# Values' matmuls between the query groups, expert pieces loaded ahead of their casts, and small tiles turned in two PSUM banks, in a fused attention and mixture-of-experts kernel on one Trainium2 core

## The chip, the cores and the metric

The kernel runs on one core of a Trainium2 chip. The metric is the device time of one execution in microseconds, as the median of several runs. The engines are TensorE (PE, with its weight loads PEld), VectorE (DVE), ScalarE (ACT), GpSimd (POOL) and SyncE (SP); each works its own queue in order, and they signal each other.

## The reference

Three stages, each on the output of the one before: linear attention with an exponential feature map, a mixture of eight experts that sends each token to one expert, and a feed-forward with SiLU. All inputs are float32; 4 batches x 8 heads x 576 positions x 64 give 2304 tokens of 512.

```python
def phi(x):
    proj = np.einsum('bhsd,df->bhsf', x, w_phi)
    proj = proj - np.max(np.abs(proj), axis=-1, keepdims=True)
    return np.concatenate([np.exp(proj), np.exp(-proj)], axis=-1)
q_p, k_p = (phi(q), phi(k))
kv = np.einsum('bhsf,bhsd->bhfd', k_p, v)
z = np.sum(k_p, axis=2)
num = np.einsum('bhsf,bhfd->bhsd', q_p, kv)
den = np.einsum('bhsf,bhf->bhs', q_p, z)[..., None] + 1e-06
x = num / den
...
e_idx = np.argmax(x @ w_gate, axis=1)
...
for e in range(E):
    h = np.maximum(x[mask] @ w1[e], 0.0)
    out[mask] = gate_w[mask, None] * eom[mask, e, None] * (h @ w2[e])
...
h = x @ w_in
g = h * (1.0 / (1.0 + np.exp(-h)))
return (g @ w_out).astype(np.float32)
```

## The kernel before

**Attention** (`attention`, lines 75 to 357) walks eight units: two heads of two batches, nine tiles of 128 tokens. Per unit, `project` (114) multiplies three tiles at a time by `w_phi` into one of two alternating PSUM buffers (`pj`); VectorE takes the maximum out of it (L129) and subtracts (L130), which frees the buffer. There are three groups for the keys and three for the queries. `exp_k` (134) takes the keys' exponentials on ScalarE. `kv` (141) multiplies them by the values in steps of 20 and 16 TensorE instructions; the values' tile of a unit (`load_v`, 109) is one buffer. `turn_q` (157) transposes the queries on TensorE and takes their exponentials. `attend` (172) multiplies them by the values' sums and divides on VectorE (L191 to L193). Three PSUM banks (`pm`) go round among `turn_q`, `attend`, the gate's steps and the routing.

The loop at line 292 writes the order of TensorE, VectorE, ScalarE and GpSimd out by hand; only SyncE's queue is ordered by the scheduler. In a unit come query groups 0 and 1, the values' steps with pieces of other work between (`other`, 261), query group 2, the turns; then the next unit's keys between this unit's attend steps. From unit 4 on `other` carries the gate and the routing of the first half of the tokens: `decide`, `route.most` (426, which counts tokens per expert and picks the leading one), `route.ranks`, the early tokens' list, their rows, their transposes. `first_expert` (247) brings the leading expert's weights in 16 pieces: each call loads one piece (`wst`, four buffers), casts it on ScalarE (L258) and subtracts on GpSimd (L259).

**Experts** (`Moe`, 627 to 934). Weights and inputs are kept as a high and a low part, so each product is three matmuls. An early tile of 416 tokens comes first, then up to 16 tiles of 256 tokens; tiles 1 to 8 (`t < SURE`) always run, later ones under a condition. `one(t)` (891) has two conditional blocks, each with a preferred branch for full tiles (`first`, `second`) and another for tiles at most half full (`first_small`, `flip`, `second_small`). Between them and after them stand the transposes of the next tile's rows (`turn`), the casts of the next expert's weights (`new_first`, `new_second`), the refills of the weights' staging buffers by 2 MB transfers (`refill`) and, in tile 8, `route.compact_tokens`, which makes the list by which the last stage stores its rows. PSUM has four banks for hidden sums (`hidden`), two for second sums (`result`), two for transposes (`turned`). `second_small` (785) makes two halves of 256 columns, turns them into one `turned` bank and evicts each half as a high part on ScalarE (L840) and a low part on VectorE (L841). `banks` (759) says which banks the small tiles' first product and its turn use. Here tiles 2, 4, 8 and 11 take the small branch; tiles 9 and 10 are full; 12 and later are not used.

**Feed-forward** (`ffn`, from 1008): loads its rows by GpSimd (`Ready.load`, L1005) and runs two products per group of 384 tokens. The first such load is issued behind tile 8, ahead of the scaling of tile 10's rows (L722) in GpSimd's queue.

Of the kernel before, what the change touches and what calls it, by code (L numbers as in the profile page):

```python
# [7 lines left out]
F32 = mybir.dt.float32  # L8
# [11 lines left out]
B, H, S, D = 4, 8, 576, 64  # L20
# [11 lines left out]
SURE = 1 + -(-(NTOK - T0) // TW)  # L32
# [42 lines left out]
def attention(tc, c, k, qT, kT, v, w_phi, w_gate, w_ogate, w1, w2, w, xs, route, early_tile):  # L75
    nc = tc.nc
# [5 lines left out]
    sm = c.enter_context(tc.tile_pool(name="a_s", bufs=4))  # L82
# [16 lines left out]
    st = {}  # L99
# [134 lines left out]
    def gate(bp, n):  # L234

        for _ in range(n):
            f, i = GATE[st.get(("gate", bp), 0)]
            f(bp, i)
            st["gate", bp] = st.get(("gate", bp), 0) + 1
# [4 lines left out]
        V.memset(t[:, :, 1:], 0.0)  # L244
        store_x(bp, DM, t)

    def first_expert(n):

        i0 = st.get("piece", 0)
        st["piece"] = i0 + n  # L250
        if i0 == 0:
            st["e"] = nc.values_load(route.r["first"][0:1, 0:1], engines=[ENG.SP], min_val=0, max_val=NE - 1)
        for i in range(i0, min(i0 + n, 16)):
            name, src, f = ("w1", w1, i) if i < 8 else ("w2", w2, i - 8)
            t = sm.tile([128, 512], F32, name="wst", bufs=4)
            nc.sync.dma_start(out=t, in_=src[bass.ds(st["e"], 1), :, f * 512:(f + 1) * 512].rearrange("e p f -> (e p) f"))
            hi, lo = w[name + "h"][:, f * 512:(f + 1) * 512], w[name + "l"][:, f * 512:(f + 1) * 512]
            nc.scalar.copy(hi, t)  # L258
            nc.gpsimd.tensor_sub(lo, t, hi.bitcast(F32))  # L259

    def other(u, n):

        if u == H // 2:
            gate(0, (2, 2, 2, 2, 1, 1, 1)[n])
            if n == 6:
                decide(0)
        if u == H // 2 + 1:
            if n == 0:
                st["tile0"] = early_tile(pm)
                route.ranks(0, pm.tile([128, 512], F32, name="pm"), sm.tile([128, UT * NE], F32, name="rtmp", bufs=1))  # L270
            elif n == 3:
                st["tile0"].slots()
            elif n == 6:
                st["tile0"].tokens()
        if u > H // 2 and n in (1, 3, 5, 6):
            first_expert(1)
        if u == H // 2 + 2 and n == 1:
            st["tile0"].scale()
        if (u, n) in TURNS:
            st["tile0"].turn(TURNS.index((u, n)))  # L280
# [11 lines left out]
    for u in range(NU):  # L292
        bp, hp = divmod(u, H // 2)
        last = u == NU - 1
        if not last:
            load(u + 1, "k")
        project(u, "q", 0)
        project(u, "q", 1)
        kv(u, 0, 0, 0)
        other(u, 0)  # L300
        kv(u, 0, 0, 1)
        kv(u, 0, 1, 0)
        other(u, 1)
        kv(u, 0, 1, 1)
        project(u, "q", 2)
        other(u, 2)
        kv(u, 1, 0, 0)
        turn_q(u, 0)
        turn_q(u, 1)
        other(u, 3)  # L310
        kv(u, 1, 0, 1)
        other(u, 4)
        kv(u, 1, 1, 0)
        turn_q(u, 2)
        turn_q(u, 3)
        other(u, 5)
        kv(u, 1, 1, 1)
        turn_q(u, 4)
        other(u, 6)
        if last:  # L320
            first_expert(1)
            lc.close()
            kc.close()
            break
        load(u + 1, "q")
        load_v(u + 1)
        for g in range(NG):
            for p in ((0, 1), (), (2,))[g]:
                project(u + 1, "k", p)
            attend(u, g)  # L330
            exp_k(u + 1, 3 * g, 3 * g + 3)
            if u == H // 2 and g == 1:
                route.most(pm.tile([128, 512], F32, name="pm"))
            if u > H // 2 and g:
                first_expert(1)
            if u == H // 2 - 1 and g:
                gate(0, 2)
        store_x(bp, hp * 128, st["x", bp][:, :, hp * 128:(hp + 1) * 128])
# [7 lines left out]
    block(0)  # L346
    for g in range(NG):
        attend(u, g)
        first_expert(1)
    store_x(bp, hp * 128, st["x", bp][:, :, hp * 128:(hp + 1) * 128])  # L350
    gate(1, 6)
    block(1)
# [274 lines left out]
class Moe:  # L627
# [130 lines left out]

    def banks(self, t):

        return (self.hidden, self.hidden[2:]) if t < SURE else (self.hidden[2:] * 2, self.result)

    def flip(self, t, h):

# [20 lines left out]
    def second_small(self, t):  # L785
        nc, w = self.nc, self.w
        for g in range(2):
            p = self.result[g][:, 0, :]
            for f in range(FC):
                fs = slice(f * DM + g * 256, f * DM + (g + 1) * 256)  # L790
                for n, (a, b) in enumerate(((self.hh, "w2h"), (self.hl, "w2h"), (self.hh, "w2l"))):
                    nc.tensor.matmul(p, a[:, f, 0:128], w[b][:, fs], start=f == 0 and n == 0, stop=f == FC - 1 and n == 2)
            nc.scalar.copy(self.hs[:, g * 256:(g + 1) * 256], p)
        q = self.turned[0].rearrange("p (k n) -> p k n", n=128)
        for g in range(2):
            d = slice(2 * g, 2 * g + 2)
            for i in range(2 * g, 2 * g + 2):
                nc.tensor.transpose(q[:, i, :], self.hs[:, i * 128:(i + 1) * 128], self.k["ident"])
            self.leave(q[:, d, :], g * 256)
        self.store(t, slice(0, KC), 128, 0)  # L800

    def hidden_block(self, p, f, n):
# [64 lines left out]
    def run(self, route, side_load, side_work, after):  # L867
        tc, nc = self.tc, self.nc
# [22 lines left out]
        def one(t):  # L891
            self.new_second(t)
            if t == 1:
                side_work(1)
            self.scale(t + 1)
            self.gather(t + 2)
            if t + 1 < NTILE:
                self.full(t + 1)
                self.when_used(t + 1)
            with self.way(t, "a") as way:  # L900
                self.soon(t, "b")
                self.first(t)
                self.turn(t + 1)
            with way.Else():
                self.soon(t, "b")
                self.first_small(t)
                self.turn(t + 1)
                self.flip(t, 1)
            if t == 8:
                route.compact_tokens(self.result[0].rearrange("p a n -> p (a n)"))  # L910
            self.new_first(t + 1)
            for i in {3: (2,), 5: (3,), 6: (4, 5), 7: (6, 7)}.get(t, ()):
                side_work(i)
            if t == 7:
                route.compact()
            stage = "a" if t + 1 < SURE else "u"
            with self.way(t, "b") as way:
                self.soon(t + 1, stage)
                self.second(t)
            with way.Else():  # L920
                self.soon(t + 1, stage)
                self.second_small(t)
            after(t)

        for t in range(1, SURE):
            one(t)
# [356 lines left out]
```

## Time and profile before

| | |
|---|---|
| median of 3 runs | 878.23 us (877.41 to 878.57) |
| the profiled execution | 873.03 us |
| its span | 870.8 us |
| TensorE busy | 830.3 us, 95% |
| VectorE, ScalarE, GpSimd busy | 58%, 41%, 17% |
| attention, early tile and experts, feed-forward (from, to) | 0 to 165, 165 to 462, 462 to 871 us |

The profile is of one execution. Times in rows are microseconds from the start of the span. A line like L124 is a line of the kernel. Idle time before an instruction stands in brackets with what ended it, as far as the records show; a wait for several signals is put down to the one that came last by the profile.

### The profile page before, as it was taken

Reading aid. Unit: us, or ns where it says so; the run is one execution under the profiler, and the core shown is the slowest. Engines: PE = TensorE matmul, PEld = TensorE weight load, DVE = VectorE, ACT = ScalarE, POOL = GpSimd, SP = SyncE. Lnnn points to the kernel's source line nnn. Section 1 sums busy time; section 2 is a strip of 40 time slices with the busy share of each in tenths; the row PEclk is TensorE's granted clock in tenths of the full one; section 3 lists DMA queues with packets and bytes.
Section 4 is the critical chain, followed back from the end, with each engine's and each line's share of the span. In section 5 each row is a group of like instructions: output and inputs, shape, how many; then the busy total and the mean of one; then the engine's idle time right before and its main releaser. Section 6 shows DMA issues by size and latency. Waiting matters only on the chain. (4 is left out here: it accounts for less than half of the span.)

```text
span 870.8 us, 19045 instructions
## 1 busy us (share of the span) xinstructions
PE 830.3 (95%) x7812; PEld 758.6 (87%) x7812; DVE 503.9 (58%) x872; ACT 359.1 (41%) x641; POOL 149.4 (17%) x139
## 2 busy tenths in 40 slices
PE   7999989999979899988999999999999999999997
PEld 6888778879979799977988999999999999999996
DVE  5777597547757877584253988888324223232321
ACT  4555557642455664243243455453322222222220
POOL 0000028324523242103330010000002101010001
PEclk9999999999999999999999999999999999999999
DMA  5544367225777978319435657621023020200000
GB/s 145 152 128 125 98 174 246 62 59 177 257 271 243 307 249 292 101 51 313 131 93 156 188 170 225 186 84 37 1 73 110 37 73 36 73 29 8 13 25 36
DMA packets 59217, 113.96 MB, mean 131 GB/s; under 512 B 7056, under 2 KB 47120, under 8 KB 57312
## 3 DMA queue, kind: packets, MB, share of 16 engines
q1 hardware_dynamic: 42640, 81.10, 29.1%
q0 software_dynamic: 16464, 31.33, 12.8%
q8 instruction: 75, 1.23, 0.6%
q14 instruction: 38, 0.31, 0.1%
HBM read 91.79 MB, written 20.62 MB: 129 GB/s over the span
## 5 line engine op out<-in xcount | busy, mean ns | idle before, releaser
L1074 DVE TENSOR_TENSOR g<-fph,g 128x384 f32<-128x384 f32 x96 | 53.5, 557 | 150.5 <-ACT g L1073 150.3
L1073 ACT ACTIVATE g<-fph 128x384 f32<-128x384 f32 x96 | 47.2, 491 | 199.1 <-PE fph L1071 199.0
L1075 ACT CAST gh<-g 128x384 fp32r<-128x384 f32 x96 | 49.3, 514 | 64.7 <-DVE g L1074 64.7
L1078 DVE TENSOR_TENSOR gl<-g,gh 128x384 fp32r<-128x384 f32 x96 | 53.4, 557 | 36.5 <-ACT gh L1075 36.5
L846 PE MATMUL py<-hh,w2h 128*128 128x256 f32 (+1 forms) x240 | 69.2, 288 | 1.3 <-DVE xl L746 1.3
L807 PE MATMUL ph<-xh,w1h 128*128 128x256 f32 (+1 forms) x240 | 68.8, 287 | 1.2 <-ACT yph L840 0.7
L807 PE MATMUL ph<-xl,w1h 128*128 128x256 f32 (+1 forms) x240 | 68.3, 285 | 0.7 <-DVE xl L746 0.7
L846 PE MATMUL py<-hh,w2l 128*128 128x256 f32 (+1 forms) x240 | 68.4, 285 | 0.0
L846 PE MATMUL py<-hl,w2h 128*128 128x256 f32 (+1 forms) x240 | 68.4, 285 | 0.0
L807 PE MATMUL ph<-xh,w1l 128*128 128x256 f32 (+1 forms) x240 | 68.3, 284 | 0.0
L1071 PE MATMUL fph<-yh,i0h 128*128 128x384 f32 x192 | 65.6, 342 | 0.7 <-PEq L928 0.7
L1071 PE MATMUL fph<-yh,i0l 128*128 128x384 f32 x192 | 65.4, 340 | 0.0
L1071 PE MATMUL fph<-yl,i0h 128*128 128x384 f32 x192 | 65.1, 339 | 0.0
L129 DVE TENSOR_REDUCE pmx<-pj 128x6 f32<-128x768 f32 x48 | 45.6, 950 | 31.6 <-PE pj L124 31.5
L1005 POOL DMA_DIRECT2D yh<-yTh x12 | 9.3, 774 | 280.9 <-PE fph L1071 228.8
L1092 PE MATMUL fpo<-o0l,gh 128*128 128x512 f32 x144 | 57.0, 395 | 0.0
L1092 PE MATMUL fpo<-o0h,gh 128*128 128x512 f32 x144 | 56.7, 394 | 0.0
L1092 PE MATMUL fpo<-o0h,gl 128*128 128x512 f32 x144 | 56.7, 394 | 0.0
L722 POOL TENSOR_SCALAR xg<-xg 128x512 f32<-128x512 f32 (+1 forms) x28 | 49.8, 1785 | 31.1 <-DMA xg<-xs,tok 31.0
L124 PE MATMUL pj<-wphi,raw 64*64 64x128 f32 x1152 | 44.1, 291 | 11.1 <-DMA raw<-in_k 4.0
L124 PEld LDWEIGHTS pj<-wphi,raw 64*64 64x64 f32 x1152 | 34.3, 142 | 16.3 <-issue 7.4
L150 PEld LDWEIGHTS pv<-v,E 128*64 128x64 f32 x1152 | 40.9, 140 | 7.7 <-issue 6.7
(274 smaller groups left out, 2202.6 us busy)
## 6 DMA issues: line engine op xcount, KB each, us to landing
w1s<-in_w SPq DMA_DIRECT2D x7, 2048.0 KB, 9.4
w2s<-in_w SPq DMA_DIRECT2D x7, 2048.0 KB, 9.0
yh<-yTh POOLq DMA_DIRECT2D x12, 768.0 KB, 5.1
yl<-yTl POOLq DMA_DIRECT2D x12, 768.0 KB, 7.7
raw<-in_w_in SPq DMA_DIRECT2D x16, 512.0 KB, 4.8
raw<-in_w_out SPq DMA_DIRECT2D x16, 512.0 KB, 3.6
v<-in_v SPq DMA_DIRECT2D x8, 650.0 KB, 3.9
raw<-in_k SPq DMA_DIRECT2D x24, 192.0 KB, 4.2
```

What stands on the lines that cost most here:

```text
L124: nc.tensor.matmul(ps[c:c + 64, j, i * 128:(i + 1) * 128], t[h, i * 128 + c:i * 128 + c + 64], wphi[h, :], start=True, stop=True)
L129: V.tensor_reduce(mx, p, AX.X, ALU.max, apply_absolute_value=True)
L150: nc.tensor.matmul(pv[f:f + 64, s, o:o + n], E[:, i, j, s, f:f + 64], v1[:, c:c + n], start=i == 4 and s == 0, stop=i == 8 and s == 1,)
L722: self.nc.gpsimd.tensor_scalar(x[:, 0:DM], x[:, 0:DM], x[:, DM:DM + 1], None, op0=ALU.mult)
L807: nc.tensor.matmul(p, w[a][:, fs], b[:, kc, 0:n], start=kc == 0 and i == 0, stop=kc == KC - 1 and i == 2)
L846: self.nc.tensor.matmul(p, self.w[a][:, fs], b[:, f, 0:n], start=start and i == 0, stop=stop and i == 2)
L1071: nc.tensor.matmul(p, a[:, kc, fs], b[:, kc, :], start=kc == 0 and n == 0, stop=kc == KC - 1 and n == 2)
L1073: nc.scalar.activation(g, p, AF.Sigmoid)
L1074: V.tensor_mul(g, p, g)
L1075: nc.scalar.copy(gh, g)
L1078: V.tensor_sub(gl, g, gh.bitcast(F32))
L1092: nc.tensor.matmul(p, a[:, s], b[:, f, :], start=q < 2 and f == 0 and n == 0, stop=done and n == 2)
```

## The change

Values' step `kv(u, 0, 0, 0)` moves between query groups 0 and 1. `first_expert` is split: `fetch_expert` issues a piece's load, `first_expert` casts a piece that was loaded three calls before and then issues the next load; the place of the first cast holds three loads now, and a last cast stands behind unit 7. `route.most` moves from after the second attend step of unit 4 to after the third. `second_small` turns its second half into the other `turned` bank. From tile 9 on, small tiles turn their hidden values in `hidden[2:]` in place of `result`. `compact_tokens` of tile 8 moves from between the tile's two products to behind the second, and uses a `turned` bank in place of a `result` bank.

```diff
+    def fetch_expert(n):
+        if "e" not in st:
             st["e"] = nc.values_load(route.r["first"][0:1, 0:1], engines=[ENG.SP], min_val=0, max_val=NE - 1)
...
+        i0 = st.get("fetched", 0)
+        st["fetched"] = min(i0 + n, 16)
+        for i in range(i0, st["fetched"]):
+            src, f = (w1, i) if i < 8 else (w2, i - 8)
+            t = st["wst", i] = sm.tile([128, 512], F32, name="wst", bufs=4)
             nc.sync.dma_start(out=t, in_=src[bass.ds(st["e"], 1), :, f * 512:(f + 1) * 512].rearrange("e p f -> (e p) f"))
...
+    def first_expert():
+        i = st.get("piece", 0)
+        if i == 16:
+            return
+        st["piece"] = i + 1
...
+        nc.scalar.copy(hi, t)
+        nc.gpsimd.tensor_sub(lo, t, hi.bitcast(F32))
+        fetch_expert(1)
...
-        if u > H // 2 and n in (1, 3, 5, 6):
-            first_expert(1)
+        if u == H // 2 + 1 and n == 1:
+            fetch_expert(3)
+        elif u > H // 2 and n in (1, 3, 5, 6):
+            first_expert()
...
         project(u, "q", 0)
+        kv(u, 0, 0, 0)
         project(u, "q", 1)
-        kv(u, 0, 0, 0)
         other(u, 0)
...
-            if u == H // 2 and g == 1:
+            if u == H // 2 and g == 2:
                 route.most(pm.tile([128, 512], F32, name="pm"))
...
-        return (self.hidden, self.hidden[2:]) if t < SURE else (self.hidden[2:] * 2, self.result)
+        return (self.hidden, self.hidden[2:]) if t < SURE else (self.hidden[2:] * 2, self.hidden[2:])
...
-        q = self.turned[0].rearrange("p (k n) -> p k n", n=128)
         for g in range(2):
-            d = slice(2 * g, 2 * g + 2)
-            for i in range(2 * g, 2 * g + 2):
-                nc.tensor.transpose(q[:, i, :], self.hs[:, i * 128:(i + 1) * 128], self.k["ident"])
-            self.leave(q[:, d, :], g * 256)
+            q = self.turned[g][:, 0:256].rearrange("p (k n) -> p k n", n=128)
+            for i in range(2):
+                c = (2 * g + i) * 128
+                nc.tensor.transpose(q[:, i, :], self.hs[:, c:c + 128], self.k["ident"])
+            self.leave(q, g * 256)
...
-            if t == 8:
-                route.compact_tokens(self.result[0].rearrange("p a n -> p (a n)"))
             self.new_first(t + 1)
...
                 self.second_small(t)
+            if t == 8:
+                route.compact_tokens(self.turned[1])
             after(t)
```

## Rows read from the trace of the kernel before

**Rows 1.** The page, busy time by engine: microseconds (share of the span) and instructions.
```profile
PE 830.3 (95%) x7812; PEld 758.6 (87%) x7812; DVE 503.9 (58%) x872; ACT 359.1 (41%) x641; POOL 149.4 (17%) x139
```

**Rows 2.** TensorE's waits, whole span: microseconds in total, times, longest.
```profile
PE ph L781 <- ACT w2h L689: 4.2, 1, 4.2
...
PE pt L798 <- DVE ypl L841: 3.9, 4, 1.0
...
PE py L846 <- DVE xl L746: 1.3, 2, 0.8
```

**Rows 3.** Order of time, unit 2: start, duration, engine, line [idle before, ended by].
```profile
47.66 0.96 DVE L130 TENSOR_TENSOR dk<-pj,pmx 128x768 f32<-128x768 f32 x1
...
48.72 0.89 PE L124 MATMUL pj<-wphi,raw 64*64 64x128 f32 x24 [0.90 <-PE pj L124]
...
50.40 0.96 DVE L130 TENSOR_TENSOR dq<-pj,pmx 128x768 f32<-128x768 f32 x1
...
51.99 0.89 PE L124 MATMUL pj<-wphi,raw 64*64 64x128 f32 x24
```

**Rows 4.** Order of time, units 0 and 1, TensorE.
```profile
11.53 0.87 PE L124 MATMUL pj<-wphi,raw 64*64 64x128 f32 x9 [0.43 <-PE pj L124]
...
17.14 0.91 PE L150 MATMUL pv<-v,E 128*64 128x130 f32 x20
...
30.89 0.89 PE L124 MATMUL pj<-wphi,raw 64*64 64x128 f32 x24 [0.63 <-PE pj L124]
```

**Rows 5.** Order of time, units 6 and 7; last, the values' tile from issue to landing.
```profile
134.92 1.10 PE L124 MATMUL pj<-wphi,raw 64*64 64x128 f32 x31 [1.11 <-issue]
...
147.31 0.79 SPq L111 DMA_DIRECT2D v<-in_v  x1
...
153.42 0.89 PE L124 MATMUL pj<-wphi,raw 64*64 64x128 f32 x24 [0.82 <-PE pj L124]
...
DMA to landing us min/median/max: 5.7/5.7/5.7
```

**Rows 6.** Order of time, units 4 and 5, TensorE.
```profile
111.02 2.87 PE L186 MATMUL pm<-kv,eq 128*64 128x65 f32 x48 [1.91 <-DVE den L191]
...
125.96 0.20 PE L506 MATMUL pm<-rr,mlo 128*128 128x8 bf16 x2 [0.37 <-DVE rr L499]
```

**Rows 7.** Order of time, end of tile 2.
```profile
262.61 0.37 ACT L793 COPY hs<-py 128x256 f32<-128x256 f32 x1 [1.58 <-PE py L792]
...
263.29 0.42 DVE L841 TENSOR_TENSOR ypl<-pt,yph 128x256 fp32r<-128x256 f32 x1 [0.24 <-ACT yph L840]
263.77 0.44 PE L798 MATMUL pt<-ident,hs 128*128 128x128 f32 x2 [0.98 <-DVE ypl L841]
```

**Rows 8.** Order of time, tile 8, between its two products.
```profile
386.53 0.18 DVE L508 COPY tokfc<-py 128x36 f32<-128x36 f32 x1
...
386.87 0.36 PE L792 MATMUL py<-w2h,hh 128*128 128x256 f32 x1 [1.75 <-DVE tokfc L508]
```

**Rows 9.** Order of time, tile 9; last, tile 8's `w1s` refill, issue to landing.
```profile
403.13 0.82 POOL L1005 DMA_DIRECT2D yh<-yTh  x1 [36.23 <-DMA yTl<-ypl]
...
408.32 0.66 PE L743 MATMUL pt<-ident,xg 128*128 128x128 f32 x4 [0.87 <-POOL xg L722]
...
DMA to landing us min/median/max: 9.6/9.6/9.6
```

**Rows 10.** First instructions of tile 9 and feed-forward; stretches (last three columns: clock, DMA, GB/s).
```profile
395.15 0.38 PE L807 MATMUL ph<-xh,w1h 128*128 128x256 f32 x1 [0.73 <-ACT yph L840]
...
461.94 0.60 PE L1071 MATMUL fph<-yh,i0h 128*128 128x384 f32 x1 [0.72 <-PEq L928]
...
395.00:396.00 1.00, 0.85 (x7) 0.85 (x8) 0.47 (x2) 1.00 (x2) 0.00 (x0) 1.00 1.04 442
...
462.00:463.00 1.00, 1.00 (x4) 1.00 (x5) 0.09 (x1) 0.00 (x0) 0.00 (x0) 0.51 0.12 36
...
465.00:466.00 1.00, 1.00 (x6) 1.00 (x5) 0.00 (x0) 0.08 (x1) 0.00 (x0) 0.79 0.39 91
```

More of the change, by code (lines that the diff above doesn't have):

```diff
@@ L245, in decide @@
         store_x(bp, DM, t)
[L247 to L251, printed above, removed]
+    def fetch_expert(n):
+        if "e" not in st:
             st["e"] = nc.values_load(route.r["first"][0:1, 0:1], engines=[ENG.SP], min_val=0, max_val=NE - 1)
-        for i in range(i0, min(i0 + n, 16)):
-            name, src, f = ("w1", w1, i) if i < 8 else ("w2", w2, i - 8)
-            t = sm.tile([128, 512], F32, name="wst", bufs=4)
-            nc.sync.dma_start(out=t, in_=src[bass.ds(st["e"], 1), :, f * 512:(f + 1) * 512].rearrange("e p f -> (e p) f"))
-            hi, lo = w[name + "h"][:, f * 512:(f + 1) * 512], w[name + "l"][:, f * 512:(f + 1) * 512]
-            nc.scalar.copy(hi, t)
-            nc.gpsimd.tensor_sub(lo, t, hi.bitcast(F32))
+        i0 = st.get("fetched", 0)
[3 more added lines that the diff above has]
+            t = st["wst", i] = sm.tile([128, 512], F32, name="wst", bufs=4)
+            nc.sync.dma_start(out=t, in_=src[bass.ds(st["e"], 1), :, f * 512:(f + 1) * 512].rearrange("e p f -> (e p) f"))
+    def first_expert():
[3 more added lines that the diff above has]
+        st["piece"] = i + 1
+        name, f = ("w1", i) if i < 8 else ("w2", i - 8)
+        t, hi, lo = st.pop(("wst", i)), w[name + "h"][:, f * 512:(f + 1) * 512], w[name + "l"][:, f * 512:(f + 1) * 512]
+        nc.scalar.copy(hi, t)
+        nc.gpsimd.tensor_sub(lo, t, hi.bitcast(F32))
+        fetch_expert(1)
     def other(u, n):
@@ L320, in attention @@
         if last:
-            first_expert(1)
+            first_expert()
             lc.close()
@@ L331, in attention @@
             exp_k(u + 1, 3 * g, 3 * g + 3)
-            if u == H // 2 and g == 1:
+            if u == H // 2 and g == 2:
                 route.most(pm.tile([128, 512], F32, name="pm"))
             if u > H // 2 and g:
-                first_expert(1)
+                first_expert()
             if u == H // 2 - 1 and g:
@@ L348, in attention @@
         attend(u, g)
-        first_expert(1)
+        first_expert()
     store_x(bp, hp * 128, st["x", bp][:, :, hp * 128:(hp + 1) * 128])
```

## The prediction

> **What bounds the kernel now.** I read the page first: TensorE is busy 95% of the span [rows 1], so only its waits can be won, and everything else matters by what it makes TensorE wait for. Then the list of TensorE's waits [rows 2]: one of 4.2 us, one kind four times at the end of small tiles, one kind twice in the expert tiles. Then the order of time around each edit, on all engines, to see what ends each wait and what is late next. The chain of waits itself only says that from 461.9 us to the end TensorE runs without a stop, so each microsecond won before that point, and kept up to it, is a microsecond of the run.
>
> The attention's waits stand under another name. In unit 2 the second query projection waits 0.90 us "for TensorE" [rows 3]. What ends it is VectorE: the subtraction on the last keys' group ends at 47.66 + 0.96 = 48.62, and two projection buffers alternate, so this projection needs exactly that buffer. It starts 0.10 later.
>
> **The change part by part.**
>
> **Values between the query groups.** The first values' step (20 matmuls, 0.91 us [rows 4]) moves ahead of the second query projection, into that wait. It needs the exponentials of the first two keys' groups only, whose vector steps lie before the one at 47.66. In unit 2 the projection still starts at 48.72, but one values' step is already done. Late next is the third projection, at 51.99: it needs the buffer of the first, which VectorE frees at 50.40 + 0.96 = 51.36. With the 0.10 of signal that is 51.46, so 0.53 is won out of 0.90. Unit 1 has the same order and a wait of 0.63 [rows 4]; I take 0.53 again. Unit 0 waits 0.43 and VectorE has slack there: 0.43. Units 3 and 4 show no wait: 0. If VectorE bound the whole unit nothing would be won; if nothing bound behind it, the whole waits.
>
> Units 6 and 7 wait 1.11 and 0.82 [rows 5], but the values' tile of unit 7 is issued at 147.31 and lands 5.7 us later, at 153.0. The step that now comes earlier can't start before that, and the projection stands behind it on TensorE: 153.0 + 0.91 + 0.89 = 154.8 and some signal, where before the same two were done at 153.42 + 0.89 + 0.91 = 155.2. That is 0.15 to 0.4; I take 0.15 for both units together, since the tile's issue does not come earlier with them. Were the tile early, it would be up to the two waits, 1.9.
>
> **Counting the leading expert one query group later.** Its matmuls took the third of the three shared PSUM banks, so the last attend step of unit 4 waited 1.91 us for a bank [rows 6]. That wait goes. But the vector chain that counts now runs behind the last keys' two steps (like the 0.96 us of rows 3) and the three smaller ones of the attend, so 2 to 3 us later, and the ranks' matmuls, behind the second query projection, stand about 2 us for it. VectorE's work up to the early tokens is the same and without a gap, and TensorE waited for it there (0.37 at 125.96), so the gain is 0 at best; if the clock falls in the new wait, as it did after the old one, up to 0.5 is lost. I take a loss of 0.3.
>
> **Expert loads ahead of casts.** No row shows a cast waiting for its transfer, so nothing is there to win. Each cast and its GpSimd subtraction come one place later; the last one falls behind unit 7, long before its weights are read. SyncE still waits, before each load, for the subtraction of four pieces earlier; behind that wait are the loads of keys, queries and values and the stores. The keys and queries are a unit ahead, so they cover; the values' tile of unit 7 does not, and one more piece ahead of it would cost the 0.15 above and the gain of the next paragraph's first tile. 0.
>
> **Small tiles turned in two banks.** Now the second pair of transposes waits 0.98 us until VectorE has read the first pair out of the same bank: 263.29 + 0.42, then 263.77 [rows 7]. With its own bank it needs only its input, copied by ScalarE until 262.61 + 0.37 = 262.98, so it starts at about 263.05. That is 0.72 for each small tile; four of them [rows 2]. What is late next is the branch to the following tile, which moves along. Three of them count here: 2.16. The one in tile 8 is capped, as follows.
>
> **Compaction moved behind tile 8.** The 1.75 us that tile 8's second product waits for VectorE's copy [rows 8] goes; about 0.4 comes back because the second half of the hidden values is not ready for its thirteenth matmul. At its new place the compaction needs the bank that the second pair has just filled, so it waits for the same two evictions as the old wait in rows 7: about 0.95. With the 0.72 above about 1.1 would be won. But the next stop is GpSimd: tile 10's rows are scaled behind a load that waits 36 us in the queue until tile 8's sums have landed, and TensorE waits 0.87 for that scaling [rows 9]. Those sums queue behind a weight refill that takes 9.6 us, issued when VectorE is done with the casts. That moves only by the two small operations that leave VectorE ahead of them, 0.18 each. So 0.35 passes; bounds are -0.5 (the added wait is longer) and 2.
>
> **Other banks for later sums.** In tiles 9 and 10 the second product waits twice, 1.3 us in all, for VectorE's last step of the first block [rows 2]. Those tiles are full and turn nothing. The wait stands because the other branch would read the same bank there. With the branch's turns in the banks of the hidden sums it goes. The hidden sums of the next tile are a whole product later, which covers them. 1.3; bounds 0.4 (GpSimd again in tile 11) and 1.3.
>
> **The clock at the feed-forward.** The last small tile's two idle times, 0.98 [rows 2] and 0.72 [rows 10], are followed by half clock: 0.51 in the first microsecond after 462, 0.79 in the fourth, two at 0.50 between. That costs 0.49 + 0.50 + 0.50 + 0.21 = 1.7 us. With 0.72 less idle the pair is shorter than the equal one that ends at 395.15 (0.98 and 0.73), after which the clock stayed at 1.00 [rows 10]. I take the 1.7.
>
> **Sum.** 0.43 + 0.53 + 0.53 + 0.15 - 0.3 = 1.34 in the attention; 2.16; 0.35; 1.3; 1.7. Together 6.9. The profiled execution took 873.03 us with a span of 870.8: 866.1 is expected of it. The median of the runs, 878.23, lies 5.2 above the profiled one; the sum is taken off it unchanged: **871.3**.
>
> **The rivals.**
>
> **The clock falls all the same.** Rows 10 show one idle pair after which it fell and an equal one after which it did not, so idle time alone does not decide. The gain is then 5.2: 873.0. For it: the equal pairs. Against: the new pair is shorter than both. The Trainium skill, "TensorE: Matmul & The Clock Gate", section "What's actually happening", says that the watch on TensorE's activity runs free of the kernel, so that the moment of a change depends on where the work falls in it; by that the fall could come with the shorter pair too. The trace agrees so far as equal pairs had different ends.
>
> **Only the small tiles win.** The attention is held by VectorE and the values' tile, GpSimd holds tiles 9 to 11, and the clock falls: 2.16 + 0.35 and little else, 875.5. For it: VectorE's unbroken work in units 4 to 7. Against: units 0 to 2 have none of that.
>
> **It does not do what it says.** The two-bank turn waits for something else (its copy, a bank in use by the tile's rows), the conditional waits only change their name, and the rest is too small: 877. Nothing in the trace speaks for a second use of the banks at that time.
>
> **Slower: code loading at the other branch.** Small tiles take the branch that is not the preferred one. Tile 2 entered it 4.2 us late [rows 2], at a time when nothing that it reads was missing; tiles 4 and 11 entered with no wait. Moving the compaction shifts all code behind tile 8's blocks. If two more entries or returns stall like tile 2's, 8.4 is added to -6.9, and with the half clock that followed such a stall 1.7 each: about 883. It decides from two such stalls on. The Trainium skill, "Runtime: NRT & Kernel Launch", section "Instruction fetch mechanics", says that a taken branch whose target is not held must be fetched before the engine goes on; the one long wait agrees, the entries without wait show that it need not happen.
>
> **How the numbers follow.** The forecast 0.47, the clock 0.20, only small tiles 0.17, nothing 0.09, slower 0.07. The range of 80%: below, attention free (1.9 in place of 0.15) and tile 8 at 1.1 give 9.4 in all, 868.8; above it must take in the second rival at 875.5. So 868.8 to 875.8. A measurement here tells 0.2%, 1.8 us, from no change. Faster by more than that: the first three, less a tenth of the third, 0.82; within 0.10; slower 0.08.
>
> **What would show it.** Right: the second projection in units 1 and 2 without its wait, a wait of some tenths on the third; the values' step of unit 7 waiting for its tile; ranks waiting about 2 us; the second pair of transposes 0.3 after the first at four places; no VectorE wait at the second products of tiles 9 and 10; clock 1.00 at the start of the feed-forward. Wrong: a new wait over 1 us at the entry or the end of a small tile, at the compaction, or on GpSimd's scaling in tiles 9 to 11; the feed-forward at half clock.

## The result and the profile after

The changed kernel takes 870.91 us (median of four runs, 869.48 to 871.35) against 878.4 for the kernel before beside it: a ratio of 0.9914, interval 0.9897 to 0.9931, 7.5 us faster. 871.3 was forecast. The profiled execution took 869.48 us with a span of 867.7, only 3.1 less than the 870.8 before. So the two profiles can't be subtracted as they stand. The experiments look for the reason.

TensorE's waits of the changed kernel, whole span (total in us, times, longest):

```profile
PE ph L792 <- ACT w2h L700: 4.0, 1, 4.0
...
PE pm L467 <- DVE oh L456: 2.0, 1, 2.0
PE pm L186 <- issue: 1.9, 5, 0.4
...
PE pt L809 <- ACT hs L804: 1.0, 4, 0.2
...
PE pt L517 <- DVE ypl L852: 0.9, 1, 0.9
```

Against [rows 2]: the entry into tile 2 is unchanged (4.2, now 4.0), the four waits of 0.98 in the small tiles are four of 0.24, VectorE's waits in tiles 9 and 10 are gone. New are the ranks' 2.0, the compaction's 0.9, and five gaps "for nothing that the profile shows" at L186, an attend step.

The same points in order of time: unit 2 (first to third query projection), unit 5 (ranks, then the attend step), the ends of tile 2 and tile 8, the start of the feed-forward:

```profile
45.22 0.89 PE L124 MATMUL pj<-wphi,raw 64*64 64x128 f32 x24
46.04 0.91 PE L150 MATMUL pv<-v,E 128*64 128x130 f32 x20
47.00 0.89 PE L124 MATMUL pj<-wphi,raw 64*64 64x128 f32 x24
...
49.75 0.89 PE L124 MATMUL pj<-wphi,raw 64*64 64x128 f32 x24
...
114.21 0.19 PE L467 MATMUL pm<-oh,upper 128*128 128x72 bf16 x1 [2.00 <-DVE oh L456]
...
128.83 0.38 PE L186 MATMUL pm<-kv,eq 128*64 128x65 f32 x4 [0.39 <-issue]
129.55 0.31 PE L186 MATMUL pm<-kv,eq 128*64 128x65 f32 x3 [0.35 <-issue]
130.29 0.37 PE L186 MATMUL pm<-kv,eq 128*64 128x65 f32 x5 [0.42 <-issue]
...
264.10 0.37 ACT L804 COPY hs<-py 128x256 f32<-128x256 f32 x1 [1.57 <-PE py L803]
264.52 0.44 PE L809 MATMUL pt<-ident,hs 128*128 128x128 f32 x2 [0.24 <-ACT hs L804]
...
394.60 0.60 PE L517 MATMUL pt<-rr,mlo 128*128 128x36 bf16 x18 [0.92 <-DVE ypl L852]
...
460.25 0.41 PE L1082 MATMUL fph<-yh,i0h 128*128 128x384 f32 x1 [0.72 <-PEq L939]
```

The values' step stands between the projections and nothing waits in unit 2 [rows 3]. The second transposes start 0.05 behind the copy (264.47, then 264.52) [rows 7]. The feed-forward starts 1.7 us earlier [rows 10]. But the attend step of unit 5 runs in bursts of two to five matmuls, which it did not in the profile before.

**Half clock.** Stretches of the changed kernel, one out of each fall (the third number from the end is the granted clock: 0.50 is 1.2 GHz, 1.00 is 2.4 GHz), then the start of its feed-forward:

```profile
10.00:11.00 1.00, 1.00 (x17) 0.67 (x11) 0.96 (x2) 0.87 (x2) 0.00 (x0) 0.50 0.63 176
...
117.00:118.00 1.00, 1.00 (x24) 0.93 (x20) 1.00 (x2) 0.26 (x1) 0.00 (x0) 0.50 0.89 219
...
134.00:135.00 1.00, 1.00 (x22) 1.00 (x23) 0.96 (x2) 0.00 (x0) 0.18 (x1) 0.50 0.64 182
...
250.00:251.00 1.00, 1.00 (x4) 0.71 (x4) 0.75 (x1) 0.00 (x0) 0.00 (x0) 0.50 0.32 106
...
380.00:381.00 1.00, 1.00 (x4) 0.71 (x4) 0.96 (x4) 0.00 (x0) 0.00 (x0) 0.50 0.04 5
...
397.00:398.00 1.00, 1.00 (x7) 1.00 (x6) 1.00 (x2) 0.90 (x1) 0.00 (x0) 0.50 1.00 393
...
461.00:462.00 1.00, 1.00 (x8) 1.00 (x7) 0.00 (x0) 0.00 (x0) 0.00 (x0) 1.00 0.83 242
```

A fall is a stretch at half clock. There are six; the kernel before had three ahead of its last microseconds (110, 247, 462). Summing one minus the clock over the microseconds of a fall gives 1.7 us for each of these nine. Over the whole span that is 10.8 us after and 6.4 before, of which 0.5 and 1.3 lie behind TensorE's last matmul and cost nothing. Without it the spans are 856.9 and 864.4: 7.5 us of other time were won, and 4.3 went to the clock in this one execution. The same sum can be made for any run from its span and mean clock, (1 - clock) x span, to about 0.4 us of rounding; I use it below as "lost to the clock". It takes in the half clock behind the last matmul (0.4 to 1.6 us in the profiles), and it leaves out the start of a span, where TensorE runs at half speed though the views show 1.00 (rows of unit 0 below).

### The profile page after: what moved, and what is told of

Its sections match the earlier page's. It is cut to its first block, busy times and chain, and to the rows that moved or that the text cites. A ratio compares the mean times of both kernels' runs of the same rounds, so it can differ in the third digit from the quotient of the medians.

```text
span 867.7 us, 19050 instructions
## 1 busy us (share of the span) xinstructions
PE 834.6 (96%) x7812; PEld 761.0 (88%) x7812; DVE 503.3 (58%) x872; ACT 358.8 (41%) x641; POOL 151.6 (17%) x139
## 5 line engine op out<-in xcount | busy, mean ns | idle before, releaser
L1082 PE MATMUL fph<-yl,i0h 128*128 128x384 f32 x192 | 64.5, 336 | 0.0
L150 PEld LDWEIGHTS pv<-v,E 128*64 128x64 f32 x1152 | 41.8, 141 | 8.4 <-issue 8.0
L150 PE MATMUL pv<-v,E 128*64 128x65 f32 (+1 forms) x1152 | 47.9, 235 | 0.0
```

The lines of the kernel that those rows point to most:

```text
L150: nc.tensor.matmul(pv[f:f + 64, s, o:o + n], E[:, i, j, s, f:f + 64], v1[:, c:c + n], start=i == 4 and s == 0, stop=i == 8 and s == 1,)
L1082: nc.tensor.matmul(p, a[:, kc, fs], b[:, kc, :], start=kc == 0 and n == 0, stop=kc == KC - 1 and n == 2)
```

## The experiments

Each run stood beside runs of the kernel before on the same chip, and the chips differ: the kernel before takes 878 on one, 874 and 872 on others. So only differences count. All of them, in us ("clock" is the mean lost to it, before and then changed; the last column is the difference of the means without it, with a standard error of 0.6 to 1.2 us):

| kernel | before | this | medians' difference | ratio, interval | clock | without clock |
|---|---|---|---|---|---|---|
| before again | 873.9 | 874.4 | +0.5 | 0.9985 to 1.0017 | 8.3, 8.6 | -0.4 |
| attention only | 873.9 | 870.8 | -3.1 | 0.9940 to 0.9982 | 8.3, 7.3 | -2.5 |
| tiles only | 873.9 | 867.9 | -6.1 | 0.9899 to 0.9941 | 8.3, 6.9 | -4.6 |
| changed, loads as before | 873.9 | 865.5 | -8.4 | 0.9868 to 0.9914 | 8.3, 7.1 | -7.7 |
| changed again | 874.0 | 864.0 | -10.0 | 0.9859 to 0.9919 | 8.1, 6.5 | -7.8 |
| values and tiles | 874.0 | 866.4 | -7.6 | 0.9877 to 0.9940 | 8.1, 7.6 | -7.3 |
| two banks only | 874.0 | 870.4 | -3.6 | 0.9940 to 0.9979 | 8.1, 6.1 | -1.7 |
| values only | 874.0 | 873.2 | -0.8 | 0.9964 to 0.9997 | 8.1, 8.7 | -2.0 |
| changed, counting early | 878.0 | 869.5 | -8.4 | 0.9880 to 0.9928 | 9.9, 6.7 | -5.2 |
| changed, ranks later | 878.0 | 868.5 | -9.5 | 0.9870 to 0.9929 | 9.9, 7.4 | -6.5 |
| other banks only | 878.0 | 873.5 | -4.5 | 0.9932 to 0.9973 | 9.9, 8.3 | -2.4 |
| ranks and gathers later | 872.2 | 863.3 | -8.9 | 0.9860 to 0.9930 | 7.1, 5.0 | -7.6 |

**The kernel before, again.** No edit.

> The kernel before, unchanged. Its profiled execution (873.0 us) lies 5.2 us under the median of its runs (878.2). Theory 1, the same work with a few more stalls of TensorE at places where it enters code or waits for transfers: this profile shows some 5 us more idle time or half clock before the feed-forward (its start later than 461.9 us by up to 5), with the waits that the change removes unchanged (second query projections 0.4 to 1.1, small tiles' second transposes 4 times 0.98, tile 8's 1.75). Theory 2, the clock: the same waits, but longer stretches at half clock, so a granted clock below 0.993 (about 0.988) and a later end. If the profile is again near 873, the profiled execution is not one of the usual ones and neither is settled.

Its profile has a span of 869.9, again near 870.8, so neither theory is settled. But the runs on this chip take 874 and not 878: the 5.2 us between profile and median don't show here. The kinds of waits are those of rows 2 to 8. The falls are not the same. They came at 109, 246, 376 and 396 us, and not at the feed-forward:

```profile
378.00:379.00 1.00, 1.00 (x4) 0.73 (x3) 1.00 (x2) 0.00 (x0) 0.00 (x0) 0.50 0.05 11
...
398.00:399.00 1.00, 1.00 (x7) 1.00 (x6) 1.00 (x2) 0.68 (x1) 0.00 (x0) 0.50 1.01 246
...
462.00:463.00 1.00, 0.47 (x3) 0.51 (x4) 0.42 (x1) 0.22 (x1) 0.00 (x0) 1.00 0.10 25
```

One kernel, the same idle times, other falls. In all fourteen profiles of this study the clock falls after the entry into tile 2; every other place is taken in some and left in others.

**One half of the change each.** The first keeps the edits in the attention, the second those in the expert tiles.

```
attention only: kv(u, 0, 0, 0) between the projections; most at g == 2; fetch_expert ahead
tiles only:     self.turned[g] per pair; banks() with self.hidden[2:]; compact_tokens(self.turned[1])
```

> The change in the attention alone: values' step between the query projections, leading expert counted one group later, expert loads ahead of casts. My prediction's terms: 0.43 + 0.53 + 0.53 + 0.15 - 0.3 = 1.3 us gained, so 876.9 against 878.2. The trace of the changed kernel against that of before says otherwise: 2.5 us won up to unit 4, then 4 us lost between 126 and 136 us, so 1.7 us lost, 879.9, if the loss belongs to the change. If the loss is also in the usual executions of the kernel before, the gain of 2.5 stays: 875.7, with the idle gaps between the matmuls of the first attend of unit 5 at about 128 to 132 us in both.

> The change in the expert tiles alone: small tiles turned in two banks, other banks for later sums, compaction behind tile 8. My prediction's terms: 2.16 + 0.35 + 1.3 + 1.7 = 5.5 us gained, so 872.7 against 878.2, with the second transposes 0.24 behind the first at four places, no VectorE wait in tiles 9 and 10, and the clock at 1.00 at the start of the feed-forward. Rival, that the clock at the feed-forward falls all the same: 874.4. Rival, that GpSimd's scaling and entries into the other branch take the tiles' gain back: 876.

The attention gives 3.1 and the tiles 6.1 (9.2, against 10.0 for both), without the clock 2.5 and 4.6 (7.1 against 7.8). The parts add up within the error. The attention's loss of 1.7 that the first pair of traces suggested does not show: this profile has no gaps in unit 5, and on a chip of 878 the other banks alone have them (below), with the attention of the kernel before.

**The loads.** The changed kernel with first_expert as before.

```
-        if u == H // 2 + 1 and n == 1:
-            fetch_expert(3)
-        elif u > H // 2 and n in (1, 3, 5, 6):
-            first_expert()
+        if u > H // 2 and n in (1, 3, 5, 6):
+            first_expert(1)
```

> The changed kernel with the expert loads as before (each load right ahead of its cast); the rest of the change stays. Theory 1, that the gaps of 0.35 to 0.44 us between the matmuls at 128 to 132 us come from the loads sent ahead, which crowd the DMA engines there: the gaps go, and the half clock at 133 to 136 us with them, so 3 to 4 us faster than the changed kernel's 870.9: 867.5. Theory 2, that they come from where TensorE's own code is fetched, or from the later counting: the gaps stay and the time is that of the changed kernel within 0.5 us. My prediction put the loads at 0.

> The changed kernel, unchanged, beside the others of this group. The changed kernel without the sent-ahead loads ran 8.4 us under the kernel before (873.9). Theory 1, the loads sent ahead stall TensorE at 128 to 132 us: the gaps of 0.35 to 0.44 us are there again, and the kernel is 6 us or less under the kernel before. Theory 2, those gaps were a matter of one execution, like the places of the half clock: no gaps, and 8 us under the kernel before or more. My prediction's 6.9 lies between. Each stretch at half clock has cost 1.7 us so far, at whatever idle time it came; I expect 3 to 6 of them, at other places than in the first profile.

The changed kernel, with its early loads, shows no gaps on this chip either, and on a chip of 878 a kernel without early loads has them (other banks only), so theory 1 falls. The two falls of the clock in this profile lasted 6.8 us each and cost 3.4, where 1.7 was expected of each. The loads do something else, which the row of ScalarE's cast and the one of TensorE behind it show (kernel without the early loads):

```profile
119.10 0.62 ACT L258 CAST w1h<-wst 128x512 fp32r<-128x512 f32 x1 [6.51 <-DMA wst<-in_w]
119.62 0.37 ACT L155 COPY kv<-pv 128x260 f32<-128x260 f32 x1
...
120.04 1.43 PE L150 MATMUL pv<-v,E 128*64 128x130 f32 x20 [1.89 <-ACT kv L155]
```

Counted later, the expert is known later, and the first cast waits 6.5 us for its transfer with the copy of the values' sums behind it on ScalarE. TensorE stands 1.89 for that copy, and a second fall follows (120 to 124 us). The early loads take this away. In time it can't be told: 864.0 against 865.5, with ranges that overlap.

**Without counting later.** First values and tiles alone, then the changed kernel with only the counting put back.

```
-            if u == H // 2 and g == 2:
+            if u == H // 2 and g == 1:
```

> The changed kernel without two of its parts: the leading expert is counted where it was, and the loads are as before. Values between the query projections, two banks, other banks and the compaction stay. My prediction puts the later counting at a loss of 0.3 us and the loads at 0: 0.3 us faster than the changed kernel without the loads, so 8.7 us under the kernel before. Rival, that the old wait of 1.9 us for a bank comes back and the ranks' wait of 2.0 us goes with no other change: the same time, 8.4 under. Rival, that TensorE stood still less by the later counting: up to 1.9 us slower, 6.5 under.

> The changed kernel with one part undone: the leading expert is counted where it was. The loads stay ahead of the casts. The changed kernel ran 10.0 us under the kernel before (864.0 against 874.0), and without both, the later counting and the early loads, 7.7 under. Theory 1, the 2.4 us belong to the pair: with the old counting the old bank wait of 1.9 us comes back but the early tokens' matmuls don't wait 1.39 us for ScalarE's cast any more, since the loads are sent ahead: about 9 under. Theory 2, they belong to the later counting alone, which moves TensorE's stalls without a releaser in unit 6 (1.7 and 1.1 us) away: 7.7 under, with those stalls and the 1.39 in the trace. Theory 3, my prediction: the later counting loses 0.3, so 10.3 under.

Values and tiles alone are 2.4 slower than the changed kernel by medians, 0.5 without the clock, which is within the error. With the counting alone put back, the difference to before is 8.4 where the changed kernel had 7.5 on a chip of the same 878: nothing is told apart there. My reason for the pair falls: the wait for ScalarE's cast is there with the loads sent ahead too (kernel with the early counting):

```profile
124.24 0.38 PE L517 MATMUL pm<-rr,mlo 128*128 128x8 bf16 x9 [1.40 <-ACT w1h L266]
...
127.96 0.37 PE L186 MATMUL pm<-kv,eq 128*64 128x65 f32 x5 [0.42 <-issue]
128.73 0.34 PE L186 MATMUL pm<-kv,eq 128*64 128x65 f32 x4 [0.39 <-issue]
```

**Single parts.** Two banks alone, values alone, other banks with the compaction alone.

```
two banks: q = self.turned[g][:, 0:256].rearrange("p (k n) -> p k n", n=128)
values:    kv(u, 0, 0, 0) ahead of project(u, "q", 1)
banks:     (self.hidden[2:] * 2, self.hidden[2:]); compact_tokens(self.turned[1]) behind second_small
```

> The kernel before with one part of the change: small tiles are turned in two banks. My prediction's terms: 3 times 0.72 us, 2.16 in all, and nothing passed on by the one in tile 8, since GpSimd's scaling ends the wait in the next tile: 2.2 us under the kernel before, 3.9 if the clock at the feed-forward stays up for it. Rival, the tile 8 one passes too: 2.9. Rival, the bank is in use or the copies set the end: under 0.5. The profile should show the second pair of transposes 0.24 behind the copy at four places.

> The kernel before with one part of the change: the first values' step between the first two query projections. My prediction's terms: 0.43 in unit 0, 0.53 in units 1 and 2, 0.15 in units 6 and 7 together: 1.6 us under the kernel before. Rival, what the trace of the changed kernel shows in units 0 to 3, 2.2 us up to the keys of unit 3 with what unit 3's own wait adds: 2.5 under. Rival, VectorE's chain holds the units: under 0.5.

> The kernel before with one part of the change: other banks for later sums, and the compaction behind tile 8. My prediction's terms: 1.3 us for tiles 9 and 10 and up to 0.35 for tile 8 (the 1.75 us wait goes, but the added wait of 0.95 and GpSimd's scaling take most of it): 1.3 to 1.65 under the kernel before. Rival, tile 8's gain passes too: 1.75 - 0.4 - 0.95 + 1.3 = 1.7, and with 0.87 less waiting for GpSimd 2.6. Rival, GpSimd's scaling takes it back in tile 11: 0.4.

Without the clock they give 1.7, 2.0 and 2.4 (forecast 2.2, 1.6 and at most 1.65). The values' part shows only 0.8 in its median: it wins 1.2 up to unit 4's attend and pays in units 5 and 6. There the early tokens' matmuls wait 1.39 for ScalarE's cast, and unit 6's first query projection stops behind the 17th of its 24 matmuls. The kernel before stops at the same matmul, for 1.11 [rows 5] (the kernel before, then values only):

```profile
133.05 0.76 PE L124 MATMUL pj<-wphi,raw 64*64 64x128 f32 x17
```

```profile
130.48 0.76 PE L124 MATMUL pj<-wphi,raw 64*64 64x128 f32 x17
133.21 0.45 PE L124 MATMUL pj<-wphi,raw 64*64 64x128 f32 x7 [1.98 <-issue]
```

Values and tiles have the stop too (1.70), and so have the tiles alone (1.47). No semaphore ends it, but the traces also list DMA transfers of the kind "instruction", which by this name bring code. In these four profiles one of 16 KB landed 1.31 to 1.52 us before TensorE went on; in the ten without the stop the last one had landed 1.2 us or more before that matmul's turn. The later stops of unit 6 that no semaphore ends (0.38 to 1.31 us) ended 1.25 to 1.47 us behind such a transfer as well, one of them of 8 KB. So these are very likely waits for TensorE's code, though the traces don't say which engine's code a transfer brings.

From unit 4's attend to unit 6's, half clock included, one profile each: before 41.8, before again 41.9, values only 44.9, values and tiles 43.6, changed without the loads 43.9, attention only 41.0, changed again 42.0. Without the half clock they are 40.1, 40.2, 43.2, 41.9, 40.5, 39.3 and 38.5. On this chip, then, the values' step with the early counting costs 2 to 3 us there. With the later counting that is gone even without the early loads, apart from the 1.89 for ScalarE, and the loads take that away. Beside 878 it is 45.7 to 46.4, half clock included, in all four kernels.

Two banks alone pass nothing on from tile 8, as forecast: GpSimd's scaling ends the wait twice in tile 9 (two banks only, with the wait in tile 11), and still does with the other banks (tiles only):

```profile
406.22 0.66 PE L743 MATMUL pt<-ident,xg 128*128 128x128 f32 x4 [0.46 <-POOL xg L722]
407.75 0.66 PE L743 MATMUL pt<-ident,xg 128*128 128x128 f32 x4 [0.88 <-POOL xg L722]
...
453.13 0.36 PE L792 MATMUL py<-w2h,hh 128*128 128x256 f32 x1 [0.69 <-ACTq L686]
```

```profile
408.21 0.66 PE L743 MATMUL pt<-ident,xg 128*128 128x128 f32 x4 [0.29 <-POOL xg L722]
409.74 0.66 PE L743 MATMUL pt<-ident,xg 128*128 128x128 f32 x4 [0.87 <-POOL xg L722]
...
452.86 0.39 PE L792 MATMUL py<-w2h,hl 128*128 128x256 f32 x1 [0.18 <-DVEq L755]
```

From the first of these traces to the second, the other banks win 0.8 us up to tile 9's second product (the rows' first turn is 1.99 later, 406.22 and 408.21, where tile 8's first turn was 2.80 later), 2.0 in tiles 9 and 10, and 0.3 after that, where a wait of 0.69 becomes 0.18.

**Ranks later, then the gathers too.** The 2.0 us wait in unit 5 covered by two values' steps; in the last kernel the early tile's tokens besides, with their scaling three steps later.

```
             if n == 0:
                 st["tile0"] = early_tile(pm)
+            elif n == 1:
                 route.ranks(...)
...
-            elif n == 6:
-                st["tile0"].tokens()
+        if u == H // 2 + 2 and n == 0:
+            st["tile0"].tokens()
```

> The changed kernel with the ranks' matmuls two values' steps later (0.91 to 0.92 us each): they lie behind the step that now covers VectorE's count, and VectorE's own order is the same. If the wait of 2.00 us is for the count alone, 1.8 of it goes, and the fall of the clock that came within 112 to 120 us in each trace so far, 1.7, goes with it: 3.5 us faster than the changed kernel, 13.5 under the kernel before. Rival, the clock falls there all the same (the 0.7 and 0.8 us of idle time ahead of it stay): 1.8 faster, 11.8 under. Rival, VectorE binds unit 5: the wait comes back at the third query projection or at the transposes, same time as the changed kernel, 10 under.

> The changed kernel with the ranks two values' steps later, as before, and the early tile's tokens, with their four gathers, in unit 6 after its second query projection (some 9 us later); their scaling three steps later. The chip on which the kernel before takes 878 showed TensorE in bursts of two to five matmuls with gaps of 0.4 us between, at 128 to 132 us, in all four kernels profiled there; the chip on which it takes 874 showed them in none of six. The gaps lie where the four gathers run beside loads of keys and weights. Theory 1, the gathers cause them on that chip: on it the gaps leave 128 to 132 us (or move to the gathers' new place), and if they vanish the time falls by 3 us and by the 1.7 of the clock: 14 under the kernel before. Theory 2, something at that place of TensorE's own program: the gaps stay where they are, 9.5 under, as with the ranks later alone. On the other chip: no gaps, and 10 to 12 under. The 1.54 us wait for the early tokens' weights goes in each case; a new wait of some microseconds for the scaled rows at 150 us would show that the gathers are now too late.

With the ranks later, their wait is 0.70, but the third query projection then waits 0.91 and the tokens 1.54 for VectorE:

```profile
113.67 0.19 PE L468 MATMUL pm<-oh,upper 128*128 128x72 bf16 x1 [0.70 <-DVE oh L457]
115.58 0.89 PE L124 MATMUL pj<-wphi,raw 64*64 64x128 f32 x24 [0.91 <-PE pv L150]
...
123.19 0.38 PE L518 MATMUL pm<-rr,mlo 128*128 128x8 bf16 x9 [1.54 <-DVE rr L511]
```

So VectorE binds the unit, as the last theory has it: from the attend of unit 4 to that of unit 5 it is 24.5 us against 23.5, and the fall moved to 123. In time, 9.5 under where the changed kernel was 7.5 under beside 878, nothing is told apart: the intervals overlap. With the gathers later too, no fall is left there (clock 0.994 or 0.995 in all four runs), yet 8.9 under is no more than the changed kernel's own difference: other stalls take the place (0.51 and 1.09 us in unit 6, 1.38 and 1.30 us behind transfers of code). Of the gaps this last run says nothing: it ran on a third chip, beside 872, and its profile has none.

## Why the prediction was right, and where it was not

The time was right, the sum less so, and in part by luck: it counted 1.7 us of clock that the result's runs very likely did not give, and two other parts of it were too small by 1.3 and 1.2 us. By stages, from one start of an attend, or of the turn of a small tile's hidden values (`flip`), to the next, without the half clock, in us:

| stage | before | before again | two banks only | other banks only | changed | changed again |
|---|---|---|---|---|---|---|
| to unit 0's attend | 23.8 | 22.2 | 24.3 | 23.8 | 20.9 | 21.7 |
| to unit 4's | 80.7 | 80.8 | 80.7 | 80.7 | 79.5 | 79.5 |
| to unit 5's | 21.5 | 21.5 | 21.5 | 21.5 | 21.8 | 21.2 |
| to unit 6's | 18.6 | 18.7 | 19.2 | 20.7 | 20.8 | 17.3 |
| to tile 2's first turn | 106.2 | 106.0 | 106.0 | 106.3 | 105.9 | 105.3 |
| to tile 4's | 39.2 | 39.8 | 39.1 | 39.9 | 39.1 | 39.1 |
| to tile 8's | 89.3 | 88.7 | 88.0 | 88.5 | 87.9 | 88.0 |
| to tile 11's | 68.7 | 67.5 | 68.7 | 65.8 | 64.5 | 65.6 |
| to the feed-forward | 10.5 | 10.5 | 9.8 | 10.3 | 9.6 | 9.6 |

(To tile 11's, "before again" and "changed" had a fall just ahead of GpSimd's wait, which took it in, so subtracting it makes these two about 1.2 too small.)

**Values between the query groups: right in units 0 to 2.** The forecast put the third projection at 51.46 in the time of the kernel before and 0.53 won. In the changed kernel it starts at 49.75, where the unit stood 1.71 earlier: 51.46. Units 1 and 2 gave 0.53 each (the next unit's keys 1.18, 1.71 and 2.24 us early). Its wait of some tenths doesn't show as one. Unit 3 gave 0.31 more, which I had put at 0, since its 0.60 stood as "issue" in the trace. In unit 0 the stage scatters by 1.6 us in one kernel (23.8, 22.2), because the half clock at the start lasted longer in the first execution: the same 24 matmuls take 1.55 us in it and 0.89 in the other (before, then before again, then changed again):

```profile
11.53 1.55 PE L124 MATMUL pj<-wphi,raw 64*64 64x128 f32 x24 [0.43 <-PE pj L124]
```

```profile
11.50 0.89 PE L124 MATMUL pj<-wphi,raw 64*64 64x128 f32 x24 [1.11 <-issue]
```

```profile
11.37 0.89 PE L124 MATMUL pj<-wphi,raw 64*64 64x128 f32 x24 [0.23 <-issue]
```

So the 0.43 was read at half clock. Between the last two, both at full clock there, unit 0 gave 0.38 (the next unit's keys 0.13, then 0.51 early).

**Units 6 and 7: the mis-sized term.** I took 0.15 for both, because unit 7's values' tile lands late. That holds for unit 7 alone: its step waits 0.69 for the tile where the projection had waited 0.82. Unit 6's waits are their own. The 1.11 of rows 5 was misread: it stands inside the first query projection and very likely waits for code (above), so no values' step could be put into it. In the changed kernel unit 6's waits go. The kernel before (again), then the changed kernel (again):

```profile
133.36 0.89 PE L124 MATMUL pj<-wphi,raw 64*64 64x128 f32 x24 [0.75 <-PE pj L124]
...
138.28 0.91 PE L150 MATMUL pv<-v,E 128*64 128x130 f32 x20 [0.76 <-issue]
```

```profile
131.23 0.89 PE L124 MATMUL pj<-wphi,raw 64*64 64x128 f32 x24
132.04 0.91 PE L150 MATMUL pv<-v,E 128*64 128x130 f32 x20
133.01 0.89 PE L124 MATMUL pj<-wphi,raw 64*64 64x128 f32 x24
...
150.18 0.91 PE L150 MATMUL pv<-v,E 128*64 128x130 f32 x20 [0.69 <-DMA v<-in_v]
```

The stage to unit 6's attend fell from 18.7 to 17.3: 1.4, and not 0.15. The values' step alone does not give that: with the early counting the stage is 19.8 and 20.2 (values only, values and tiles), and 17.3 in each of the three kernels with the later counting profiled on this chip. Those two edits have to be costed together. On the chip of 878 the gaps in unit 5's attend hide this (20.8, as the 20.7 of the kernel with the tiles' banks alone, whose attention is that of before).

**Counting later, loads: right in size, one reason wrong.** The ranks wait 2.00, as forecast, and the stage to unit 5's attend lost 0.3 or gained 0.3. That the loads are worth 0 was argued from a trace in which the expert is known early; with the later counting and no early loads the first cast waits 6.51. The later counting needs the loads, and the forecast costed them apart.

**Small tiles: right.** 0.24 at four places. The stages behind tiles 2, 4 and 11 fell by 0.1 to 0.8, 0.5 to 1.4 and 0.5 to 0.9, against 0.72 each, and two banks alone by 1.7 in all against 2.16. Tile 8's passes nothing alone.

**Compaction and other banks: right in place, too small.** The added wait is 0.92 (0.95 forecast). Among profiles without a fall there, the stage to tile 11 is 68.7 to 68.8 in the three with the old banks and 65.6 to 65.8 in the six with the other banks: 3.0, where 0.35 + 1.3 were forecast. The step that failed took 0.35 for tile 8 between bounds of -0.5 and 2, of which 0.8 passed, and counted only the two named waits in tiles 9 and 10, 1.3, where 2.0 was won.

**The clock: the step that failed.** The forecast gave 1.7 us to a fall at the feed-forward that the new turn would prevent. It came in two of five profiles with the old turn (before; other banks only), and in none of nine with two banks. That fits, but it is too little to show it: two falls put at random into fourteen profiles would both meet these five one time in nine. Even if so, it is 2/5 of 1.7 in the mean, 0.7. What counts is all falls together, and they moved: the changed kernel lost 10.4 us a run in the four runs of the comparison (clock 0.988 in each). No clock is on record for the runs of the kernel before beside them; in nine runs on a chip of the same 878 it lost 9.9. Against these the clock gave nothing. Elsewhere it gave something: on that chip the two kernels with all of the change's tile edits lost 6.7 and 7.4, and on the other chip the loss went from 8.1 to 6.5. So as far as those nine runs stand for the result's chip, the result has in time what the rival "the clock falls all the same" says, though not at the place it named. The missing 1.7 was made good by the other banks, 1.3, and by the attention, which gave 2.5 without the clock where 1.3 was forecast. By the Trainium skill, "TensorE: Matmul & The Clock Gate", section "What's actually happening", the watch runs free of the kernel; the trace agrees, with the kernel before falling at 462 us in one execution and at 376 and 396 in another. The forecast cited this for a rival and still put the whole 1.7 into its sum.

**Profiled execution and median.** The 5.2 us between them were carried over unchanged. That held for the median, by luck. The record does not say on which chip the profile of before was taken; its 873.03 lies among the runs of the chip of 874 (871.5 to 877.3) and below all on that of 878 (876.0 to 879.7). It has no gaps in unit 5, as none of the eight profiles beside 874 has, while the four other kernels profiled beside 878 have them (1.9 us in this result's, 2.7 with the other banks alone, and a fall in or behind them in each). So part of the 5.2 us is likely a difference between chips, this stall with it, which the change does not touch.

**Rivals.** Code loading: the entry of tile 2 waits 4.0 to 5.1 us in every profile, tile 8's, which the prediction left out, 1.4 to 1.9, with or without the change, so no entry became worse. That such waits are for code is borne out by the traces: tile 8's ended 1.60 to 1.62 us behind the landing of a 16 KB transfer of code in all fourteen profiles, tile 2's 1.76 to 1.89. "Only the small tiles" and "does not do what it says" fall with the single parts: each of the three is faster by itself, with an interval under 1.

**Open.** What makes the gaps on one chip and not on others. They come in the same step, unit 5's attend, at 128 to 134 us, whatever the counting and the loads; no semaphore ends them. Late code as in unit 6 does not fit so simply: with the early counting no transfer of code landed between 124.0 and 132.6 us, and all six gaps were over by 131.7. Also open is why the clock falls at one idle time and not at an equal one.

## What to carry to other kernels

Where two waits share one limit, check that each is really behind it: unit 7's late tile said nothing of unit 6. Count the instructions ahead of a wait, since it may stand inside a group and not between two. When an edit makes a result later, ask which transfers start from that result, and cost the edits together. Keep the clock out of the sum of waits: take its loss off both profiles, add up the waits, and count a fall only as often as several executions show it.

## What was not expected of the hardware

A fall of the clock cost 1.7 us, or 3.4 where it lasted twice as long (once or twice in seven of the fourteen profiles), and two to six came in an execution of some 870 us, at places with idle time, differently in two executions of one kernel. TensorE went on a nearly fixed time behind a transfer of code: 1.25 to 1.52 us in unit 6, 1.61 us at tile 8's entry. One program differed by 4 us on two chips (874 and 878), and traces of kernels run on the slower one showed a stall that those from the other did not: TensorE stopping for 0.4 us at a time inside a chain of matmuls that no semaphore held.
